# Runs of keys copied by GpSimd for two pairs of an attention + FFN kernel, with a replanned order

## The chip, the cores and the metric

The kernel runs on 1 core of one Trainium2 chip. The metric is the device time of one execution in microseconds (us): the time of the whole program on that core, as the median of several executions. The profiled execution also has a span, from its first to its last instruction; the time of the execution is a little longer than its span.

## What is computed

```python
# q, k, v: (4, 8, 768, 64); x: 3072 tokens x 512; w_in: 512 x 2048; w_out: 2048 x 512
k_sum = k.reshape(B, H, nb, 32, D).max(axis=3)      # nb = 24 blocks of 32 keys
v_sum = v.reshape(B, H, nb, 32, D).mean(axis=3)
scores_l = scale * q @ k^T, masked to |i - j| < 16
scores_s = scale * q @ k_sum^T + log(32)
a = softmax(concat([scores_l, scores_s]))
attn = a @ concat([v, v_sum])
x = attn as 3072 tokens x 512
h = x @ w_in
r = maximum(h, 0)
out = (r * r) @ w_out
```

Each query sees a window of near keys and one maximum per block of 32 keys. The attention's output feeds a squared-ReLU FFN. Everything is float32.

## The kernel before

**Tiling.** The 3072 tokens are cut into 48 groups of 64 queries (g = 0 to 47; 12 groups per batch), and from group 8 on two groups form a *pair* that is handled together: pair n holds groups 2n and 2n + 1, so pair 4 (the fifth) is groups 8, 9 and pair 5 (the sixth) is groups 10, 11. Both still belong to the first batch. Eight groups form a unit of 512 tokens; the FFN runs unit by unit (u = 0 to 5) over 16 slices f of the hidden size. Units 0 and 1 use plain products (L1345 for h, L1369 for the output); units 2 and 3 (L1655, then L1987) and 4 and 5 (L1806, then L1987) use products in Strassen's manner, with sums of weights kept in DRAM (`scr_s`, `scr_a`, `scr_i`, `scr_t`). Each FFN matrix is split into a high and a low float32r part, so a slice takes 12 matmuls of 128x512 in either direction.

**Attention.** `first_attention` handles groups 0 to 7 one by one: scores into PSUM, softmax on VectorE (DVE) and ScalarE (ACT), four transposes on TensorE (PE, L1007), then the values product (L1148). The block maxima (`kb[:, :, :24]`) must stand just ahead of a group's near keys, so GpSimd (POOL) moves them along after every group (`move`, L874, the planner's task KC); the next group's scores wait for that. Pairs are scored by `pair_scores` (L866): 8 heads x 2 halves x 2 groups, 32 products. For batches 1 to 3 the keys lie in DRAM as runs of 88 columns (32 near keys, 24 maxima, 32 near keys, and so on; kG), so a product reads 88 columns in one. For batch 0 (pairs 4 and 5) the maxima and the near keys lie apart, and `pair_keys` gives two pieces: 24 columns of maxima and 64 (or 2x32) near ones. In the order printed below a product is one MATMUL; the trace counts two records for each of them.

After its scores a pair's softmax runs on DVE and ACT, a DVE transpose fills `ta`, four DMAs store it (`turn<-ta`, L1116, task TW), two fetch it in another layout (`a<-turn`, L1124, task TR), and `visit` multiplies it with the values `v` (L1148). There are two buffers for `v` and two for `q`: the loads for the next pair can only start when the former pair's product has read them (`v<-vS`, L789, four DMAs per pair; `q<-qW`, L770, two).

**Order.** Nothing is ordered by hand. Every step is a task with an engine, a key, a cost, what it comes after and which buffers it takes; `Plan.order` simulates the five engines and emits the tasks in the order in which it starts them. The keys come from tables of numbers (`V_LEAD`, `Q_LEAD`, `VISIT_AT`, `KEEP_AT` and so on). Each engine then runs its own instructions in that order, so an instruction that waits holds back all that follow on its engine. All large transfers are issued by one queue, SyncE's (SP); in the program each DMA there waits, besides for its buffers, for the landing of the one eight places before it. The planner before models a transfer as size / 350 GB/s + 1.9 us after the one before, with a table of lateness (`FIRST_LATE`, `LATE`, `V_LATE`, `TR_LATE` and others).

**Weights of the products.** The chunks for L1987 (256 KB each, `w<-scr_a` and `w<-scr_s`, L1955, task CL) go through eight buffers, `wc`. These are places in converted weights, and in unit 2 the last slices of w_in pass through the same eight (`w<-scr_i`, L1606). A chunk load waits until the product that used its buffer is done.

The lines of before that the prediction names: L603 (block maxima of batch 0, DVE), L874 (move, POOL), L796 (copies of sums, POOL), L1281 and L1295 (conversion of weights on ACT), L1014 (copy of a transposed group, ACT), L1574 (`scr_t<-ci`, a store that waits for DVE), L1955, L770, L789.

Of the kernel before, what the change touches and what calls it, by code (L numbers as in the profile page):

```python
# [20 lines left out]
P = 128  # L21
# [42 lines left out]
)  # L64
Q_LEAD = (
# [3 lines left out]
)  # L69
K_LEAD = 73.42, -9.39, -21.49  # L70
TURN_LEAD = (
    1.51, 4.56, 10.36, 0.83, 0.32, -8.81, 19.45, 17.4, -0.53, 9.71, 8.55, -3.09, -4.94, -6.08, -5.46, -8.9, 0.58,
    20.88, 25.32, 5.2, 8.61, 23.24, 12.81, 19.17,
)
HOST_LEAD = (
    12.28, 4.72, 24.43, 38.91, 32.55, 26.28, 29.81, 14.47, -2.7, 5.84, 12.88, 18.8, 17.55, 14.9, 24.8, 22.66,
    16.06, 19.05, 26.89, 29.23, 21.55, 15.39, 32.19, 34.21, 42.91, 20.4, 27.32, 21.21, 36.11, 17.94, 3.66, -12.09,
)
CHUNK_LEAD = 21.45, 27.16, 28.13, 33.44
BLOCK_LEAD = 2.026  # L80
T0 = 28.0
SLOW = 6.007
STEP = 5.855
LEAD = 1.289
FIRST_STEP = 4.02, 3.16
BLOCK_STEP = 1.201
PRODUCT_STEP = 1.32, 1.53, 1.23, 1.04
A0 = 8.649
A1 = 1.909
B0 = 12.893  # L90
B1 = 2.229
HALF_AT = 31.92, 32.59
SECOND = 0.868
IN_AT = 182.63, 270.39, 82.72, 80.5, 255.98, 198.36, 397.3, 399.37
EARLY_SUM = 20.914
# [5 lines left out]
FIRST_LAG = 21.218  # L101
ONE_EXP = 1
LAG = 1.549
# [3 lines left out]
FV_LEAD = -0.72  # L107
FV1_LEAD = -8.476
# [3 lines left out]
TR_LATE = 1.732  # L112
V_LATE = 0.738
FIRST_W_LATE = 2.5
SOON_X = 1.804
SOON_W = 0.262
FIRST_S_KEY = -70.0
FIRST_VM = -60.0, 1.5, 2.5
IL_LATE = 2.513
SUMS_AT = 304.121  # L120
# [72 lines left out]
class Plan:  # L193
# [3 lines left out]
    HOP, DMA_LATENCY, DMA_RATE = 0.12, 1.9, 350e3  # L197
    OWN_LATENCY = 2.5
# [9 lines left out]
    def add(self, name, engine, cost, emit, key, after=(), take=(), use=(), size=0, begin=0.0, behind=None, late=0.0):  # L208
        t = Task(name, engine, cost, emit, key, [a for a in after if a is not None], list(take), list(use), size, begin)
        t.behind, t.late = behind, late  # L210
        t.index = len(self.tasks)
        self.tasks.append(t)
        for b in t.take + t.use:
            b.users.append(t)
        return t

    def order(self):
# [13 lines left out]
        events, n, pipe = [], 0, 0.0  # L231
# [19 lines left out]
        while events:  # L251
# [12 lines left out]
            for e, tasks in ready.items():  # L264
# [1942 lines left out]
```

## Time and profile before

| | |
|---|---|
| median of 3 runs | 591.32 us (589.09 to 592.77) |
| profiled execution, its own time | 589.62 us |
| its span | 587.9 us |
| PE busy | 569.5 us (97%) |
| DVE busy | 438.7 us (75%) |
| ACT busy | 361.7 us (62%) |
| POOL busy | 22.7 us (4%) |
| TensorE clock granted, mean | 0.997 of full speed |
| DMA moved | 156.20 MB, mean 266 GB/s |

PE is the engine to read: it is busy nearly all the time, so what shortens the kernel is fewer matmuls or less time in which PE has nothing to do. A busy time of matmuls is modelled at its ends, and they overlap: in a steady stream a 128x512 matmul shows 0.39 us while the next one starts some 0.227 us later (4 in 1.07 us, 12 in 2.72 us). Idle time on PE stands in square brackets in a timeline, with what ended it.

### The profile page before, as it was taken

The numbers are of one execution on the slowest core, as the hardware profiler recorded it, in microseconds if no ns is written. First come the engines' busy times: TensorE is split into PE (matmuls) and PEld (weight loads), VectorE is DVE, ScalarE is ACT, GpSimd is POOL, SyncE is SP. The second block draws the span as 40 slices with busy tenths as digits, with TensorE's granted clock in tenths as the row PEclk, the third lists the DMA queues.
The fourth block names the chain that finished last, engine by engine and source line by source line (L and its number), as shares of the span: only waits on it lengthen the run. The fifth ranks groups of instructions, "written<-read, shape, count | busy, mean of one in ns | idle before, by whom it ended". The sixth has DMA issues, their size and how long they took to land.

```text
span 587.9 us, 12572 instructions
## 1 busy us (share of the span) xinstructions
PE 569.5 (97%) x4614; PEld 463.9 (79%) x4614; DVE 438.7 (75%) x731; ACT 361.7 (62%) x825; POOL 22.7 (4%) x76
## 2 busy tenths in 40 slices
PE   8879999999999999999899999999999999999997
PEld 6677888888888888888677877788888888788885
DVE  5879999787874787776787978899935623897653
ACT  2979896766654546474663657565547856755542
POOL 4700000000000000000000010000000000000000
PEclk9989999999999999999999999999999999999999
DMA  8995888989699558989998998996899865467672
GB/s 306 369 394 168 294 271 283 316 291 302 222 277 384 177 143 258 341 273 330 353 307 259 291 286 267 296 275 209 248 334 374 280 197 159 148 192 234 195 228 98
DMA packets 101517, 156.20 MB, mean 266 GB/s; under 512 B 9888, under 2 KB 61088, under 8 KB 101456
## 3 DMA queue, kind: packets, MB, share of 16 engines
q1 hardware_dynamic: 101200, 155.00, 81.6%
q8 instruction: 37, 0.61, 0.4%
q0 software_dynamic: 256, 0.39, 0.2%
q14 instruction: 24, 0.20, 0.1%
HBM read 110.40 MB, written 44.56 MB: 264 GB/s over the span
## 4 chain that ended last, share of the span: by engine, by line
PE 75%; DMA 16%; SPq 3%; DVE 3%; ACT 2%; issue 1%; DVEq 0%
PE o L1987 17%; PE o L1369 14%; PE h L1345 14%; PE o L1806 12%; PE end L1987 7%; PE h L1655 5%; DMA raw<-wW 3%; PE x L1148 3%; DMA w<-scr_a 3%; PE att L866 2%; DMA ci<-scr_i 2%; DMA v<-vS 2%; DMA qvpa_lent<-vF 2%; DMA scr_i<-w 1%; DMA q<-qW 1%; DMA fv_lent<-vS 1%
## 5 line engine op out<-in xcount | busy, mean ns | idle before, releaser
L1971 ACT CAST gh<-g 128x512 fp32r<-128x512 f32 x112 | 69.5, 623 | 59.7 <-PE o L1987 29.7
L1976 DVE TENSOR_TENSOR gl<-g,gh 128x512 fp32r<-128x512 f32 x112 | 75.7, 687 | 20.0 <-ACT gh L1971 19.9
L1987 PE MATMUL o<-gh,w 128*128 128x512 f32 x320 | 86.6, 392 | 2.5 <-DMA w<-scr_a 2.5
L1345 PE MATMUL h<-xh,w 128*128 128x512 f32 x240 | 74.8, 392 | 0.8 <-DVE w L1298 0.8
L1987 PEld LDWEIGHTS o<-gh,w 128*128 128x128 f32 x320 | 59.4, 188 | 15.7 <-ACT gh L1971 3.3
L1655 PE MATMUL h<-xh,w 128*128 128x512 f32 x224 | 70.0, 394 | 0.4 <-ACT r L1665 0.4
L1369 PE MATMUL o<-w,gh 128*128 128x512 f32 x240 | 61.6, 393 | 0.0
L1345 PEld LDWEIGHTS h<-xh,w 128*128 128x128 f32 x240 | 44.7, 188 | 10.7 <-DVE w L1298 1.2
L1369 PEld LDWEIGHTS o<-w,gh 128*128 128x128 f32 x240 | 44.6, 188 | 9.6
L1067 ACT ACTIVATE p<-p,nm 128x88 f32<-128x88 f32 x120 | 42.9, 359 | 14.1 <-DVE nm L1061 14.1
L1987 PE MATMUL o<-gl,w 128*128 128x512 f32 x160 | 49.3, 389 | 0.0
L1655 PEld LDWEIGHTS h<-xh,w 128*128 128x128 f32 x224 | 41.4, 188 | 9.9 <-ACT r L1665 0.8
L1345 PE MATMUL h<-xl,w 128*128 128x512 f32 x120 | 46.7, 389 | 0.0
L1655 PE MATMUL h<-xl,w 128*128 128x512 f32 x112 | 43.6, 389 | 0.0
L1665 ACT ACTIVATE r<-h 128x512 f32<-128x512 f32 x32 | 19.1, 595 | 36.9 <-PE h L1655 35.3
L1987 PEld LDWEIGHTS o<-gl,w 128*128 128x128 f32 x160 | 30.0, 188 | 6.3
L1806 PE MATMUL o<-w,w 128*128 128x512 f32 x140 | 34.5, 390 | 0.0
L1987 PE MATMUL end<-gh,w 128*128 128x512 f32 x128 | 34.5, 390 | 0.0
L1354 ACT ACTIVATE r<-h 128x512 f32<-128x512 f32 x30 | 17.9, 597 | 26.3 <-PE h L1345 26.2
L1369 PE MATMUL o<-w,gl 128*128 128x512 f32 x120 | 33.6, 389 | 0.0
L1964 DVE TENSOR_TENSOR g<-g 128x512 f32<-128x512 f32 x48 | 32.5, 684 | 0.8
L1806 PEld LDWEIGHTS o<-w,w 128*128 128x128 f32 x140 | 26.2, 188 | 5.9 <-DVE u L1838 0.5
(212 smaller groups left out, 1051.4 us busy)
## 6 DMA issues: line engine op xcount, KB each, us to landing
raw<-wW SPq DMA_DIRECT2D x32, 512.0 KB, 6.9
w<-scr_s SPq DMA_DIRECT2D x64, 256.0 KB, 3.2
w<-scr_a SPq DMA_DIRECT2D x48, 256.0 KB, 3.2
w<-scr_i SPq DMA_DIRECT2D x38, 256.0 KB, 5.0
scr_t<-ci SPq DMA_DIRECT2D x16, 512.0 KB, 5.9
turn<-ta SPq DMA_DIRECT2D x80, 96.0 KB, 3.7
a<-turn SPq DMA_DIRECT2D x40, 192.0 KB, 3.9
w<-scr_t SPq DMA_DIRECT2D x28, 256.0 KB, 5.4
```

The costliest lines, as they stand in the source:

```text
L1067: nc.scalar.activation(x, x, AF.Exp, bias=nm.tile[:, n : n + 1], accum_out=nm.tile[:, H + n : H + n + 1])
L1148: nc.tensor.matmul(x_of(i)[h % 2 * D : (h % 2 + 1) * D, h // 2, :], lhsT=v_bufs[g].tile[:rows, h * D : (h + 1) * D], rhs=av[:rows, 2 * c : ...
L1345: nc.tensor.matmul(cut(h), lhsT=lhs.tile[:, k * P : (k + 1) * P], rhs=rhs[:, k, c0 : c0 + n], start=(i == 0), stop=(i == 3 * KT - 1),)
L1354: t2 = add(f"RL{name}", "ACT", act, lambda: nc.scalar.activation(cut(r), cut(h), AF.Relu), due + 3, [t1], take=[r], use=[h])
L1369: nc.tensor.matmul(o_of(o, t), lhsT=terms[i][0].tile[:, (t - t0) * P : (t - t0 + 1) * P], rhs=terms[i][1].tile, start=(first and i == 0), ...
L1655: nc.tensor.matmul(h.tile, lhsT=lhs.tile[:, k * P : (k + 1) * P], rhs=rhs[:, k, c0 : c0 + TU], start=(i == 0), stop=(i == 3 * KT - 1),)
L1665: t2 = add(f"RL{name}", "ACT", 0.56, lambda: nc.scalar.activation(r.tile, h.tile, AF.Relu), due + 3, [t1], take=[r], use=[h])
L1806: nc.tensor.matmul(o.tile[:, bank], lhsT=chunk.tile[:, w * HALF + d * P : w * HALF + (d + 1) * P], rhs=xs[y][d], start=starts and i == 0, ...
L1964: lambda x=x, ins=ins, op=op: nc.vector.tensor_tensor(out=x.tile, in0=ins[0].tile, in1=ins[1].tile, op=op),
L1971: f"GH{s}_{n}", "ACT", 0.54, lambda x=x, gh=gh: nc.scalar.copy(out=gh.tile, in_=x.tile), due - 4, ready,
L1976: lambda x=x, gh=gh, gl=gl: nc.vector.tensor_tensor(out=gl.tile, in0=x.tile, in1=gh.tile.bitcast(F32), op=ALU.subtract),
L1987: nc.tensor.matmul(o[d].tile if isinstance(o, tuple) else o.tile[:, d], lhsT=chunk.tile[:, w * HALF + d * P : w * HALF + (d + 1) * P], rhs ...
```

## The change

Three things are changed.

1. **Runs of keys.** For pairs 4 and 5, `first_run` lets GpSimd copy near keys and maxima into runs of 88 columns, as the other batches have them: four copies per pair (task KR). Those of pair 4 go to free columns behind the keys, once the four maxima (L603) are there; those of pair 5 go over the front of the keys, once groups 0 to 3 are scored and moved. `pair_keys` then gives one piece for each product.
2. **The planner.** It no longer models a transfer by one rate and a table of lateness. A DMA takes 0.44 us to issue, at most eight are open at a time, each costs by its count of packets and their size over 16 engines, with 1.2 us before and 1.0 us behind. The `late` numbers go, `dmas=(count, KB)` comes.
3. **The order.** All tables of numbers are new, so every engine's order is new.

```diff
-    HOP, DMA_LATENCY, DMA_RATE = 0.12, 1.9, 350e3
-    OWN_LATENCY = 2.5
+    HOP, HOP_PE = 0.13, 0.22
+    ENGINES, QUEUED, DMA_ISSUE = 16, 8, 0.44
+    PACKET, PER_KB = 0.006, 0.044
+    BEFORE, BEHIND = 1.2, 1.0
+    OWN_LATENCY = 4.5
...
+                if e == "SP" and len(landed) >= self.QUEUED and landed[-self.QUEUED] > now + 1e-9:
+                    free[e] = landed[-self.QUEUED]
...
-                elif t.size:
-                    pipe = max(pipe, end) + t.size / self.DMA_RATE
-                    end = pipe + self.DMA_LATENCY + t.late
+                if e == "SP":
+                    end, (count, kb) = now, t.dmas
+                    work = t.size / 1024 / kb * (self.PACKET + self.PER_KB * kb) / self.ENGINES / count
+                    for _ in range(count):
+                        if len(landed) >= self.QUEUED:
+                            end = max(end, landed[-self.QUEUED])
+                        end += self.DMA_ISSUE
+                        pipe = max(pipe, end + self.BEFORE) + work
+                        landed.append(pipe + self.BEHIND)
...
+    def first_run(pair, free):
+        lo = keys[:, NPAIR * (NB + S) + SQ :][:, : NPAIR * FIRST_RUN].rearrange("p (n k) -> p n k", n=NPAIR)
+        x = first_runs[pair] = lo if free else kb[:, :, NB : NB + FIRST_RUN]
+        k0 = NB + 2 * TQ * pair - WINDOW
...
+        def copy():
+            nc.gpsimd.tensor_copy(out=x[:, :, :SQ], in_=near[:, :, k0 : k0 + SQ])
+            nc.gpsimd.tensor_copy(
+                out=view(x, [[RUN, 2], [1, 2 * SQ]], SQ + NB), in_=view(near, [[2 * SQ, 2], [1, 2 * SQ]], k0 + SQ)
+            )
+            for i in range(2):
+                nc.gpsimd.tensor_copy(out=x[:, :, i * RUN + SQ : i * RUN + SQ + NB], in_=kb[:, :, :NB])
...
     def pair_keys(g, p, half, rows):
 
         b, w = divmod(g, NW)
-        if b:
-            at = w * RUN + half * SQ
-            return [((0, [[1, COLS]]), kg[rows, p, at : at + COLS])]
-        k0 = NB + TQ * w - WINDOW + half * SQ
-        near = keys[rows, p * (NB + S) + k0 : p * (NB + S) + k0 + HALF_W]
-        sums = kb[rows, p, :NB]
-        if half:
-            return [((0, [[1, NB]]), sums), ((NB, [[1, HALF_W]]), near)]
-        return [((SQ, [[1, NB]]), sums), ((0, [[SQ + NB, 2], [1, SQ]]), near.rearrange("p (i k) -> p i k", i=2))]
+        x, at = (kg, w * RUN) if b else (first_runs[g // 2], g % 2 * RUN)
+        return x[rows, p, at + half * SQ : at + half * SQ + COLS]
...
+    def key_runs():
+        for i, pair in enumerate(range(UG // 2, NW // 2)):
+            after = [t_S[3][0], t_KC[3]] if i else []
+            t_KR[pair] = [add(f"KR{pair}", "POOL", 1.25, first_run(pair, not i), RUNS_AT[i], [*t_K[0], t_ends, *after], begin=RUNS_AT[i])]
...
-IN_AT = 182.63, 270.39, 82.72, 80.5, 255.98, 198.36, 397.3, 399.37
+IN_AT = 230.45, 178.82, 256.9, 245.39, 276.31, 334, 389.48, 426.44
```

**What moves: PE at the end of the first eight groups.** `att` is the values product of a group, `t_` a group's transposes, `o_67<-kb,q` the scores of pair 4, `h_0a` the first half-width matmuls of the FFN. Before, with the scores' last two rows at the top:

```order
L866 MATMUL o_67<-kb,q_375 32x24
L866 MATMUL o_67<-kb,q_375 32x64
L1148 MATMUL att<-qvpa_lent 64x64 x8
L1007 MATMUL t_648<-first,qvpa_lent 128x128 x4
L1007 MATMUL t_659<-first,qvpa_lent 128x128 x4
L1148 MATMUL att<-qvpa_lent 64x64 x16
L1345 MATMUL h_0a<-xh,w_0_677 128x256 x2
```

and now:

```order
L1040 MATMUL t_558<-first,qvpa_lent 128x128 x4
L892 MATMUL o_67<-kb,q_383 32x88 x16
L892 MATMUL o_67<-kb,q_386 32x88 x16
L1181 MATMUL att<-qvpa_lent 64x64 x8
L1040 MATMUL t_619<-first,qvpa_lent 128x128 x4
L1378 MATMUL h_0a<-xh,w_0_538 128x256 x2
...
L1040 MATMUL t_656<-first,qvpa_lent 128x128 x4
L1181 MATMUL att<-qvpa_lent 64x64 x16
L1378 MATMUL h_1a<-xh,w_1_662 128x256 x2
```

The scores of a pair are 32 products instead of 64, and the twelve matmuls of `h_0a` stand ahead of the last group's transposes and values product instead of behind them.

**What moves: POOL at the start.** `kb<-kb 128x4x24` at L874 (now L900) are the moves of the maxima, the first of them after group 0's scores. Before:

```order
L586 MEMSET a_80 32x2x256 x2
L932 MEMSET qvpa_lent 128x4x10 x4
L1037 MEMSET p_79 128x8x8
L932 MEMSET qvpa_lent 128x4x10 x4
L874 COPY kb<-kb 128x4x24 x3
```

and now:

```order
L596 MEMSET a_80 32x2x256 x2
L965 MEMSET qvpa_lent 128x4x10 x3
L1070 MEMSET p_79 128x8x8
L965 MEMSET qvpa_lent 128x4x10
L866 COPY kb<-kb 128x4x32
L867 COPY kb<-kb 128x4x2x64
L871 COPY kb<-kb 128x4x24 x2
L900 COPY kb<-kb 128x4x24
```

The four copies of pair 4's run stand ahead of the first move; those of pair 5 stand at the end of POOL's work for the first groups.

**What moves: SP around the first chunks of products.** `kb<-kG` are the keys of the last batch (four DMAs of 544 KB), `w<-scr_i` the last slices of w_in, `w<-scr_a` the chunks. Before:

```order
L789 DMA v_78<-vS 64x512
L599 DMA kb<-kG 128x1088 x4
L1955 DMA w_952<-scr_a_106 128x512
L1955 DMA w_952<-scr_a_107 128x512
L1116 DMA turn_90<-ta_3439 32x3x256 x4
L1508 DMA scr_i_118<-w_908 128x1024
L1955 DMA w_956<-scr_a_108 128x512
L1955 DMA w_956<-scr_a_109 128x512
L1574 DMA scr_t_134<-ci_0_3248 256x2x256
L1574 DMA scr_t_134<-ci_1_3361 256x2x256
L1955 DMA w_1068<-scr_a_110 128x512
```

and now:

```order
L609 DMA kb<-kG 128x1088 x4
L1157 DMA a_80<-turn_87 96x2x256 x2
L799 DMA v_77<-vS 32x512
L799 DMA v_77<-vS 64x512
L1639 DMA w_910<-scr_i_126 128x512
...
L1607 DMA scr_t_132<-ci_1_3241 256x2x256
L1639 DMA w_840<-scr_i_129 128x512 x2
L1149 DMA turn_90<-ta_3369 32x3x256 x4
L1989 DMA w_910<-scr_a_106 128x512
L1989 DMA w_910<-scr_a_107 128x512
```

The keys of the last batch no longer stand directly ahead of the first chunk; between them are now nine other rows, seven loads of w_in's halves among them. They may be loaded once the scores of the pair before are done; between those and the first scores that read them stood 78 wide matmuls on PE, and now stand 84.

## Rows read from the trace of the kernel before

**Rows 1.** Busy time by stretch: us, busy us (instructions) of each engine, PEclk, DMA share, GB/s.
```profile
0.00:36.87 36.87, 29.42 (x486) 22.61 (x486) 25.07 (x61) 21.23 (x80) 17.61 (x66) 0.98 0.96 347
260.00:404.50 144.50, 138.65 (x1320) 111.40 (x1318) 119.22 (x199) 84.80 (x198) 3.09 (x6) 1.00 0.93 290
404.50:588.00 183.50, 179.06 (x792) 147.22 (x788) 114.49 (x177) 105.28 (x176) 0.00 (x0) 1.00 0.70 221
```

**Rows 2.** Waits of PE between 260 and 404 us: total us, times, longest.
```profile
PE o L1987 <- DMA w<-scr_a: 2.5, 2, 1.6
PE att L866 <- DMA q<-qW: 1.1, 1, 1.1
PE x L1148 <- DMA v<-vS: 1.0, 2, 0.6
PE x L1148 <- DMA w<-scr_i: 0.8, 1, 0.8
```

**Rows 3.** Timeline of PE: start, duration, line, operation [idle before, releaser].
```profile
63.95 1.67 PE L866 MATMUL att<-kb,q 64*32 64x24 f32 x128
104.78 0.96 PE L866 MATMUL att<-kb,q 64*32 64x88 f32 x64
```

**Rows 4.** Timeline of PE, end of the first eight groups.
```profile
35.59 1.35 PE L1148 MATMUL att<-qvpa_lent 118*64 118x64 f32 x22 [1.64 <-issue]
36.87 0.80 PE L1345 MATMUL h_0a<-xh,w 128*128 128x256 f32 x2
```

**Rows 5.** Busy time by stretch (as Rows 1) while ACT works on groups 1 to 7.
```profile
15.60:33.60 18.00, 14.89 (x352) 11.74 (x354) 14.57 (x40) 16.35 (x67) 10.29 (x24) 1.00 1.02 370
```

**Rows 6.** Timeline of ACT near the end of the first groups.
```profile
30.23 0.72 ACT L1281 ACTIVATE t<-raw 128x512 f32<-128x512 f32 x1
32.54 1.09 ACT L1014 COPY qvpa_lent<-t 128x512 f32<-128x512 f32 x2
33.52 0.62 ACT L1295 CAST w<-t 128x512 fp32r<-128x512 f32 x1
```

**Rows 7.** Timelines of DVE and POOL in the first 25 us.
```profile
9.65 0.94 DVE L603 TENSOR_REDUCE kb<-kb 128x24 f32<-128x768 f32 x1
11.15 0.27 POOL L874 COPY kb<-kb 128x96 f32<-128x96 f32 x1 [3.53 <-PE o L832]
17.89 1.72 POOL L796 COPY qvpa_lent<-fv_lent 24x512 f32<-24x512 f32 x3
23.72 0.64 DVE L996 TENSOR_TENSOR qvpa_lent<-qvpa_lent,nm 128x472 f32<-128x472 f32 x1
23.77 0.72 POOL L874 COPY kb<-kb 128x96 f32<-128x96 f32 x1 [0.64 <-PE o L832]
```

**Rows 8.** Timeline of PE: the scores of group 1.
```profile
11.98 0.63 PE L832 MATMUL o<-kb,qvpa_lent 64*64 64x118 f32 x16
```

**Rows 9.** Timeline of PE at a wait for queries and one for values.
```profile
312.03 1.02 PE L866 MATMUL att<-kb,q 64*32 64x88 f32 x64 [1.13 <-DMA q<-qW]
374.81 1.39 PE L1148 MATMUL x<-a,v 128*64 128x64 f32 x32 [0.62 <-DMA v<-vS]
```

**Rows 10.** Timeline of SP's issues at the same places (duration: of the issues).
```profile
286.57 1.36 SPq L1574 DMA_DIRECT2D scr_t<-ci  x2
288.02 4.80 SPq L1955 DMA_DIRECT2D w<-scr_a  x5
305.49 1.44 SPq L770 DMA_DIRECT2D q<-qW  x2
```

**Rows 11.** Issue to landing of q (250 to 345 us, 14 DMAs) and v (300 to 345, 9).
```profile
DMA to landing us min/median/max: 3.3/4.3/6.4
...
DMA to landing us min/median/max: 4.7/5.3/6.7
```

**Rows 12.** Timeline of PE: the last two visits of before, 24 wide matmuls apart.
```profile
396.75 1.15 PE L1148 MATMUL x<-a,v 128*64 128x64 f32 x32
403.50 1.15 PE L1148 MATMUL x<-a,v 128*64 128x64 f32 x32
```

More of the change, by code (lines that the diff above doesn't have):

```diff
@@ L100 @@
 )
-FIRST_LAG = 21.218
+FIRST_LAG = -16.679
 ONE_EXP = 1
-LAG = 1.549
+LAG = 2.227
 PLAIN = 2
@@ L206, in __init__, with add @@
         self.tasks = []
-    def add(self, name, engine, cost, emit, key, after=(), take=(), use=(), size=0, begin=0.0, behind=None, late=0.0):
+    def add(self, name, engine, cost, emit, key, after=(), take=(), use=(), size=0, begin=0.0, behind=None, dmas=(1, 2)):
         t = Task(name, engine, cost, emit, key, [a for a in after if a is not None], list(take), list(use), size, begin)
-        t.behind, t.late = behind, late
+        t.behind, t.dmas = behind, dmas
         t.index = len(self.tasks)
@@ L878, in keys_of @@
         b, w = divmod(g, NW)
-        return [t_QL[g]] + ([t_KC[g - 1]] if 0 < g < UG else [t_K[b][p] for p in pairs])
+        return [t_QL[g]] + ([t_KC[g - 1]] if 0 < g < UG else t_KR[g // 2] if not b and g >= UG else [t_K[b][p] for p in pairs])
     def first_attention(g):
@@ L915, in first_pair @@
         t_s = add(
-            f"S{both[1]}", "PE", 1.1, lambda: pair_scores(both), wanted(both[0]) - 15,
-            keys_of(both[0], range(NPAIR)) + [t_QL[both[1]], t_ends], take=s_bufs[g], use=[q_bufs[g] for g in both],
+            f"S{both[1]}", "PE", 0.75, lambda: pair_scores(both), wanted(both[0]) - 15,
+            keys_of(both[0], range(NPAIR)) + [t_QL[both[1]]], take=s_bufs[g], use=[q_bufs[g] for g in both],
         )
@@ L1126, in pair_softmax @@
         t_w = add(
-            f"TW{g}", "SP", 1.75, store, due - 8.5, [t_t], take=[d], use=[ta], size=6 * P * DM
+            f"TW{g}", "SP", 1.75, store, due - 8.5, [t_t], take=[d], use=[ta], size=6 * P * DM, dmas=(4, 1),
         )
@@ L1131, in pair_softmax @@
             t_z.append(add(f"AZ{g}", "POOL", 1.1, lambda: clear_a(a.tile), fetch_at - 8, take=[a], begin=fetch_at - 20))
-        t_a = add(f"TR{g}", "SP", 0.8, fetch, fetch_at, [t_w, t_clear, *t_z], take=[a] * (not t_z), use=[d] + [a] * len(t_z), size=6 * P * DM, behind=last_of("turn", None), late=TR_LATE if both[0] >= NW * 2 else 0.0)
+        t_a = add(f"TR{g}", "SP", 0.8, fetch, fetch_at, [t_w, t_clear, *t_z], take=[a] * (not t_z), use=[d] + [a] * len(t_z), size=6 * P * DM, behind=last_of("turn", None), dmas=(2, 1))
         last_of("turn", t_a)
@@ L1215, in visit @@
         t_v = add(
-            f"V{both[-1]}", "PE", 0.54 * n + 0.11 * (n == 1) + (0.36 if then and then[0] >= NW else 0.49) * len(then) + 0.4 * bool(block_sums), products, due, deps,
+            f"V{both[-1]}", "PE", 0.54 * n + 0.11 * (n == 1) + 0.36 * len(then) + 0.4 * bool(block_sums), products, due, deps,
             take=take, use=use,
@@ L1536, in combine_in @@
             if kept:
-                t = add(f"IL{p}_{k}", "SP", 0.45, load, due - 8 + 0.1 * k, [t_WI[f]], take=[x], size=8 * P * DM, begin=due - 14, behind=behind, late=IL_LATE)
+                t = add(f"IL{p}_{k}", "SP", 0.45, load, due - 8 + 0.1 * k, [t_WI[f]], take=[x], size=8 * P * DM, begin=due - 14, behind=behind, dmas=(1, 4))
                 t_claim.append(t)
@@ L1580, in combine_in @@
             t4 = add(f"IW{p}_{k}", "DVE", 0.6, low, due + 3 + 0.1 * k, [t3], use=[pair[k]])
-            ts.append(add(f"IS{p}_{k}", "SP", 0.45, store, due + 4 + 0.1 * k, [t4], use=[pair[k]], size=8 * P * DM))
+            ts.append(add(f"IS{p}_{k}", "SP", 0.45, store, due + 4 + 0.1 * k, [t4], use=[pair[k]], size=8 * P * DM, dmas=(1, 1)))
         t_IN[p] = ts
```

131 lines of the change are left out of this document (69 added, 62 removed), and 12 rows, old and new, of tables (Q_LEAD, V_LEAD).

## Prediction

> **What bounds the kernel now.** I read the busy time by stretch first. PE is the engine that decides, but not in the same way everywhere [rows 1]. In the first 36.87 us it handles 486 small matmuls and follows ACT and DVE. From there on the wide matmuls run one behind another, and in the last stretch, from 404.50 us on, all 786 of them stand in one block: 786 x 0.227 = 178 us of the 179.06 that PE is busy. Nothing the new order does there can gain anything. Between 260 and 404.5 us the picture is another: PE loses 5.85 us (144.50 less 138.65) while the DMA engines are 93% busy. Who was late says the list of PE's waits for that stretch [rows 2]: chunks of weights 2.5 us, queries 1.1, values 1.0, and a further 0.8 at a values product that hangs on the same queue of loads. Every one ends on a DMA. What can be gained is therefore in three places: the first 37 us, these waits, and the matmuls that are saved.
>
> Both programs have the same 2,136 wide and 48 half-width matmuls by their orders, so only what lies between those counts.
>
> **The change, term by term.** The sum is made against the profiled execution's own 589.62 us (span 587.9); the three runs have their median 1.70 us higher, so a gain is counted from the low end of them.
>
> *Scores of pair 5.* 64 products become 32, with twice the columns or more. The trace has both forms: pair 5 takes 1.67 us now, a pair of a later batch 0.96 [rows 3]. 24 and 64 columns cost as much for each product as 88. The block stands alone between wide matmuls, so the difference is on the path: **-0.7**. Pair 4's scores lie in the first stretch and are in its term.
>
> *GpSimd's copies.* Pair 4's copies wait for the fourth maximum, which DVE ends at 9.65 + 0.94 = 10.6 us [rows 7]; in the new DVE order it stands one place earlier, ahead of a 0.40 us subtraction, so about 10.3. Their prices: 96 columns 0.27 us, 512 columns 1.72 / 3 = 0.57 [rows 7]; four copies of 128, 512, 96 and 96 columns come to 0.3 + 0.57 + 2 x 0.27 = 1.4 us, until 11.7. Behind them stands the first move, which ran at 11.15 [rows 7]: it comes 0.55 us late and ends at about 12.0. Who waits for it is group 1's scores, and these started at 11.98 because other products (sums of values) stand ahead of them on PE in both orders [rows 8]. So the copies cost **0.0**, covered by those products; without that cover 0.55. Pair 5's copies stand behind all moves, some 30 us ahead of their use, and cost nothing.
>
> *The end of the first groups.* Before, the last values product has a hole of 1.64 us in its middle for which the trace names no releaser, and the wide stream starts at 36.87 [rows 4]. Now the twelve half-width matmuls of `h_0a`, 1.4 us, run ahead of the last transposes, in time that PE spent waiting. In return ACT must convert that slice's weights earlier: one rebias (0.72) and two casts (0.62 each) move ahead of the last group's copy, 1.96 us, and that copy ended at 32.54 + 1.09 = 33.6 [rows 6]. ACT was busy for 16.35 of the 18 us before [rows 5], so 1.65 us of the work may fall into its idle time: the copy ends between 33.9 and 35.6. I take 34.5. The values product follows in 1.15 us, so PE enters the stream at 35.8 with 1.4 us of it done: 36.87 - 35.8 + 1.4 = 2.5 us, less 0.3 for one more change between small and wide matmuls and 0.2 for my rounding: **-2.0**. Best, with all idle time filled, -3.0; worst, with none filled and the 1.64 us hole again, +0.7.
>
> *Chunks.* The 2.5 us come from SP, not from bandwidth alone. The first chunk was issued right behind 2.2 MB of keys; a later one was issued at 288.02, behind two `scr_t` stores at 286.57 that wait for DVE [rows 10]. Now the keys stand far ahead, and the buffer of the first chunk is free 3 x 12 wide matmuls and a pair (8.2 + 2.2 us) before its use; before, it was 8.2. The worst landing of a q load there was 6.4 [rows 11]. I take **-2.2** of the 2.5, with 0 and 2.5 as bounds.
>
> *Queries.* The loads that made PE wait 1.13 us at 312.03 [rows 9] were issued at 305.49 [rows 10], some 2.7 us after their buffer was free, behind a store and two chunks. PE has the same 30 wide matmuls between the two pairs now, but SP has only `turn` and `scr_t` stores ahead, which may wait too. **-0.7** of 1.1 (bounds 0 and 1.1).
>
> *Values in the middle.* The four loads of one visit were split around weights and fetches; now they stand together. **-1.0** of the 1.2 us that remain of the 1.0 and 0.8 without the wait at 374.81 [rows 2, 9] (bounds 0 and 1.2).
>
> *New narrow gaps.* The new order sets some visits closer. The last two are 18 wide matmuls apart (4.1 us) and were 24, which took 403.50 - 396.75 = 6.75 us without a wait [rows 12]; two others are 24 apart where 30 brought the wait of 0.62 us at 374.81 [rows 9]; queries get 24 wide matmuls at two places that had 36. A visit's loads take four issues, about 2.2 us, and then 4.7 to 6.7 [rows 11]; from the release in the visit to the next one there are 4.9 us at the tightest place. With landings near the lower bound, as late as this stage is: 0.7 + 0.5 + 0.5 = **+1.7**. Bounds 0 and +7.5 (the second rival).
>
> The planner's rule itself costs no time on the chip.
>
> Sum: 589.62 - 0.7 - 2.0 - 2.2 - 0.7 - 1.0 + 1.7 = **584.7 us**, 1.1% under the median.
>
> [...]
>
> **The rivals.**
>
> *Waits come back in other places (slower than before).* One mechanism: in the busy stage loads land at the slow end. The point is a landing above 4.8 us for queries: 24 wide matmuls and the change are 5.7 us, two issues take 0.9. At 6.4 us (and 5.8 for values) the places cost 0.6 + 2.0 + 1.8 + 3.1 = 7.5 instead of 1.7, and the chunks lose their 2.2 again: 584.7 + 5.8 + 2.2 = 592.7. For it: 93% busy DMA engines [rows 1] and those very landings [rows 11]. Against it: the last gap of 24 went without a wait [rows 12].
>
> *The waits only move.* The planner's new prices do not fit the chip better, and as much is lost in the middle as before; the saved scores and the start remain: 589.62 - 0.7 - 2.0 = 586.9. For it: SP issues in order, and the stores ahead of the loads still wait for DVE.
>
> *All waits go.* Landings near the lower bounds of [rows 11] and the start at its best: -1.7 for the gaps, -0.9 for the remains of three terms, -1.0 for the start: 581.1.
>
> *GpSimd and DVE hold each other up.* A move took 0.72 us instead of 0.27 where it met a DVE multiplication of two SBUF tiles that took 0.64 [rows 7]. If each of the four copies meets one, they take 4 x 0.45 = 1.8 us more, the first move ends at 13.8 and not at 12.0, and the scores and all behind them start that much later: 584.7 + 1.8 = 586.5. Against it: up to 11.7 us DVE does reductions and subtractions that read PSUM. [...]
>
> **How the numbers follow.** Chances: forecast 0.45 (its own range 581.5 to 587.5), slower rival 0.18, all waits go 0.17, waits only move 0.14, the port 0.06. Under 578 I see 0.07, above 592 about 0.12, so the range is 578 to 592. What differs by less than 1% a measurement of this kernel hardly tells from no change. Faster by over 1% is below 585.4: two thirds of the forecast's chance, all of the third rival and some of the rest, 0.53. Slower by over 1% is above 597.2: only the slow mechanism with more places than I counted, 0.07. The rest, 0.40, is the same.
>
> **What would show it.** In the changed kernel's trace pair 5's scores take about 0.96 us and 64 records. The first move on POOL ends by 12.0 us and group 1's scores start at 12.0. The wide stream without a break starts near 35.8 us and not after 37.5. In PE's waits `w<-scr_a` falls under 0.5 us and `q<-qW` under 0.5; the waits for `v<-vS` stand in the last visits and are about 1.5 us. The last block of wide matmuls takes 178 to 179 us as before, so its start tells the whole gain: about 400 instead of 404.6. The prediction is wrong if new waits on DMA in the middle add up to more than 4 us, if ACT ends the last group's copy after 36 us, or if the hole in the first groups turns out to come with every execution.

## The result and the profile after

The changed kernel took 582.93 us in the median of 4 runs (581.41 to 583.19), the kernel before 592.05 of 4 (589.09 to 593.68): a ratio of 0.985, interval 0.980 to 0.989. Forecast were 584.7 us, range 578.0 to 592.0. Two later groups of runs of the same two kernels gave 0.987 (0.982 to 0.993) and 0.986 (0.982 to 0.990). The profiled execution is one of 582.88 us with a span of 581.1; against 587.9 that is 6.8 us less. The medians lie 9.1 us apart; the profiled execution of before was one of the shorter ones (589.62).

Busy time by stretch of the changed kernel, columns as in [rows 1]:

```profile
0.00:35.02 35.02, 28.82 (x434) 22.00 (x434) 26.15 (x64) 21.99 (x82) 20.23 (x74) 1.00 0.96 348
260.00:399.40 139.40, 136.88 (x1229) 110.47 (x1227) 113.47 (x189) 81.59 (x189) 3.07 (x6) 1.00 0.92 288
399.40:581.00 181.60, 176.61 (x779) 144.90 (x774) 112.58 (x175) 103.73 (x174) 0.00 (x0) 1.00 0.73 220
```

The wide stream goes through without small matmuls from 35.02 us on, where it started at 36.87 [rows 1], and twelve of its matmuls are done by then. In the middle stretch PE lost 5.85 us and now loses 139.40 - 136.88 = 2.52. PE's four largest waits from 60 to 399.4 us (total us, times, longest), which answer to [rows 2]:

```profile
PE att L892 <- DMA q<-qW: 0.9, 1, 0.9
PE o L2021 <- DMA w<-scr_a: 0.9, 1, 0.9
PE h L1688 <- ACT r L1698: 0.7, 1, 0.7
PE h L1688 <- ACT fv L759: 0.4, 1, 0.4
```

The timeline of PE at the marks by which the stages are told apart below (answers to [rows 3, 4, 12]):

```profile
34.41 0.69 PE L1181 MATMUL att<-qvpa_lent 118*64 118x64 f32 x16 [0.25 <-ACT qvpa_lent L1047]
35.02 0.51 PE L1378 MATMUL h_1a<-xh,w 128*128 128x256 f32 x2
...
60.23 0.96 PE L892 MATMUL att<-kb,q 64*32 64x88 f32 x64
...
398.37 1.15 PE L1181 MATMUL x<-a,v 128*64 128x64 f32 x32
399.45 1.19 PE L2021 MATMUL o<-gh,w 128*128 128x512 f32 x4
```

Pair 5's scores are 64 records of 0.96 us in all; they were 128 of 1.67. To compare programs with different orders I cut each trace at two equal counts of wide matmuls: the end of the 132nd (the start of the small products behind it, 63.95 before, 60.23 now), and the point with 786 left (404.58 before; now 399.45 less 12 x 0.227 = 396.73, as the last visit has 774 behind it in the new order and 12 are counted over). The stages by this cut, us, for all traces taken (one trace for each row; the programs below before_again are explained with their experiments):

| kernel (span) | to the 132nd | middle | rest | stop of PE without a releaser |
|---|---|---|---|---|
| before (587.9) | 63.95 | 340.63 | 183.33 | 1.64 at 33.95 |
| before_again (593.0) | 62.98 | 346.67 | 183.35 | 1.37 at 33.89 |
| chunks_first (588.5) | 63.45 | 341.81 | 183.27 | 1.37 at 33.76 |
| keys_only (586.9) | 61.33 | 342.27 | 183.30 | none |
| order_only (585.4) | 62.99 | 337.86 | 184.52 | 1.93 at 34.21 |
| fewer_warm (583.2) | 62.48 | 336.71 | 184.03 | 0.53 at 35.93 |
| split_runs (584.4) | 62.58 | 337.03 | 184.77 | 1.66 at 34.07 |
| pair5_old (586.4) | 60.44 | 342.64 | 183.31 | 1.86 at 64.32 |
| h0a_late (582.7) | 60.93 | 337.25 | 184.54 | none |
| after (581.1) | 60.23 | 336.50 | 184.36 | none |
| after_again (583.5) | 61.28 | 338.31 | 183.87 | 0.29 at 30.68 |
| after_third (585.0) | 60.95 | 338.88 | 185.12 | none |
| queries_early (582.3) | 60.35 | 337.90 | 184.09 | none |
| fixed (580.4) | 60.56 | 336.37 | 183.48 | none |

So of the 6.8 us between the two profiled executions 3.7 came before the 132nd wide matmul and 4.1 in the middle, and 1.0 was given back at the end.

What makes the middle long or short can be read from the same traces. Take from it PE's waits (idle times of over 0.1 us) and half of the time at a granted clock of 0.50 (an estimate of what that clock costs: in before three half-width matmuls took 0.64 us from 38.11 us on, at 0.50, and 0.36 from 41.19 us on, at 1.00), and 332.8 to 334.9 us are left in all fourteen. Waits and clock together come to 5.8, 12.6 and 7.7 us in three traces of the old order (before, before_again, keys_only), to 3.0 in order_only and to 3.1, 5.3 and 6.0 in the three of the changed kernel. So the middle's gain is in PE's waits and in what the clock costs behind some of them, and it differs by microseconds from one execution to the next.

### The profile page after: what moved, and what is told of

It is laid out like the page before. It is cut to its first block, busy times and chain, and to the rows that moved or that the text cites. A ratio compares the mean times of both kernels' runs of the same rounds, so it can differ in the third digit from the quotient of the medians.

```text
span 581.1 us, 12287 instructions
## 1 busy us (share of the span) xinstructions
PE 566.4 (97%) x4486; PEld 459.8 (79%) x4486; DVE 438.0 (75%) x731; ACT 359.3 (62%) x825; POOL 25.3 (4%) x84
## 4 chain that ended last, share of the span: by engine, by line
PE 78%; DMA 16%; DVE 4%; SPq 1%; issue 1%; ACT 0%; DVEq 0%
PE o L2021 17%; PE o L1402 15%; PE h L1378 14%; PE o L1840 13%; PE end L2021 8%; PE h L1688 5%; PE x L1181 3%; DMA raw<-wW 3%; PE att L892 2%; DMA w<-scr_i 2%; DMA kb<-kG 2%; DMA ci<-scr_i 1%; DMA fv<-vT 1%; DMA fv_lent<-vS 1%; DMA qvpa_lent<-vF 1%; DMA w<-scr_a 1%
## 5 line engine op out<-in xcount | busy, mean ns | idle before, releaser
L1402 PE MATMUL o<-w,gh 128*128 128x512 f32 x240 | 61.7, 393 | 0.0
L1402 PEld LDWEIGHTS o<-w,gh 128*128 128x128 f32 x240 | 44.5, 188 | 9.5
L1840 PE MATMUL o<-w,w 128*128 128x512 f32 x140 | 34.6, 390 | 0.0
L2021 PE MATMUL end<-gh,w 128*128 128x512 f32 x128 | 34.5, 390 | 0.0
L1402 PE MATMUL o<-w,gl 128*128 128x512 f32 x120 | 33.5, 389 | 0.0
```

Of the source, the lines that this page charges most:

```text
L1402: nc.tensor.matmul(o_of(o, t), lhsT=terms[i][0].tile[:, (t - t0) * P : (t - t0 + 1) * P], rhs=terms[i][1].tile, start=(first and i == 0), ...
L1840: nc.tensor.matmul(o.tile[:, bank], lhsT=chunk.tile[:, w * HALF + d * P : w * HALF + (d + 1) * P], rhs=xs[y][d], start=starts and i == 0, ...
L2021: nc.tensor.matmul(o[d].tile if isinstance(o, tuple) else o.tile[:, d], lhsT=chunk.tile[:, w * HALF + d * P : w * HALF + (d + 1) * P], rhs ...
```

## The experiments

The theory at the start was that of the prediction: the order gains, by filling time in the first groups and by loads that come earlier, and the copies save 0.7 us and pair 4's part. Its rivals were that a stop of the first trace was an accident, and that waits only move.

**before_again and after_again: a second trace of each.** No edit.

> The kernel before, unchanged, for a second trace. Theory A, the stops come from the order: the last values product of the first groups has its hole of 1 to 2 us again, the wide stream starts at 36.5 to 37.2 us and its first 2 us run at a granted clock of 0.50, there is a wait of about 0.9 us on DVE near 50 us, and the two waits for chunks of weights between 280 and 296 us come to 2 to 3 us. Theory B, the hole is an accident of one execution: the stream starts near 35.2 us at full clock, and the span is about 585 us.

> The changed kernel, unchanged, for a second trace. Theory A, the gain belongs to the order: stream from 35.0 us (within 0.3), no half clock, waits of TensorE on DMA between 260 and 399 us of 1.0 to 3.0 us, a wait of 0.8 us on DVE at about 429 us, ratio 0.982 to 0.988. Theory B, the first trace was a lucky one: waits on DMA of over 4 us in that stretch and a ratio above 0.990.

Measured: before_again 590.39 us, ratio to the other runs of before 0.998 (0.996 to 1.001); after_again 583.47 us, 0.987 (0.982 to 0.993). The stop came again, at the same place of the program; timeline of PE of before_again:

```profile
33.36 0.53 PE L1148 MATMUL att<-qvpa_lent 118*64 118x64 f32 x10 [0.42 <-DVE xl L1235]
35.26 0.86 PE L1148 MATMUL att<-qvpa_lent 118*64 118x64 f32 x22 [1.37 <-issue]
36.05 0.50 PE L1345 MATMUL h_0a<-xh,w 128*128 128x256 f32 x2
```

The stop comes with the program; the low clock behind it doesn't come every time: at 37 to 40 us the granted clock was 0.64 in the first trace of before and 1.00 in the second (and 0.61 from 36 to 40 us in chunks_first below, which has the order of before in this stage). The middle is no constant either: 340.63 and 346.67 us in the two traces of before, with other waits and, in the second, with the granted clock at 0.50 from 289.5 to 292.9 us and at 0.54 from 357.5 to 361 us. PE's five largest waits between 260 and 410 us in before_again:

```profile
PE h L1655 <- ACT r L1665: 2.5, 2, 1.4
PE o L1987 <- DMA w<-scr_a: 1.8, 1, 1.8
PE x L1148 <- DMA w<-scr_i: 1.7, 1, 1.7
PE x L1148 <- DMA a<-turn: 1.3, 2, 0.8
PE x L1148 <- DMA v<-vS: 0.7, 1, 0.7
```

The queries, 1.1 us in [rows 2], are not among them. What I took for the price of an order was one draw of it.

**keys_only and order_only: the two halves of the change, one at a time.** keys_only is before with the copies put in by hand, everything else in the old order. order_only has the new order, with nothing copied:

```diff
-t_KR[pair] = [add(f"KR{pair}", "POOL", 1.25, first_run(pair, not i), RUNS_AT[i], ...)]
+t_KR[pair] = [add(f"KR{pair}", "POOL", 1.25, lambda: None, RUNS_AT[i], ...)]
```

and `pair_keys` and the products of before.

> The order of before, with the copies added (pair 4's ahead of the first move, pair 5's behind the last) and the two pairs scored in 32 products of 88 columns each. By the forecast pair 5 saves 0.7 us on the path, pair 4 saves 0.9 us of TensorE's time in a stretch that follows ScalarE, of which 0 to 0.9 reaches the end: 0.7 to 1.6 us, ratio 0.997 to 0.999. By the rival in which GpSimd and VectorE hold each other up, the first move ends at 13.8 us, group 1's scores start 1.8 us later, and the time is 1.1 us above before.

> The order of the changed kernel, but without the copies: pairs 4 and 5 are scored from the keys as they lie, in 64 and 128 products as before. If the gain is the order's: the changed kernel's time and 0.7 to 1.6 us, ratio to before 0.984 to 0.990. If the copies carried more than their 0.7 us, above 0.992.

Measured: keys_only 589.50 us, ratio 0.9965 (0.993 to 0.9995); order_only 586.91 us, 0.993 (0.991 to 0.995), beside 591.68 of before and 583.47 of the changed kernel on the same chip. By the medians the copies are worth 2.2 us in the old order and 3.4 in the new, where 0.7 to 1.6 was expected. Each alone is loose (the interval of keys_only is 0.3 to 3.9 us). The table says where: keys_only has no stop and is at its 132nd wide matmul at 61.33 us, order_only has one of 1.93 us and is there at 62.99, no earlier than before_again. PE of keys_only, then the scores of pair 4 in before (with the copies they take 0.96 us):

```profile
30.37 0.69 PE L1165 MATMUL att<-qvpa_lent 118*64 118x64 f32 x16 [1.41 <-ACT xh L1249]
...
33.35 1.15 PE L1165 MATMUL att<-qvpa_lent 118*64 118x64 f32 x32 [0.42 <-DVE xl L1252]
```
```profile
28.35 1.84 PE L866 MATMUL o<-kb,q 64*32 64x24 f32 x128
```

The product behind pair 4's scores starts at 30.37 us, where it was 30.44 in before: PE waits for ACT instead, so the shorter scores alone gain nothing here. What is gained in this stage is the stop, which stood inside the last values product and is gone from it.

But order_only stops at another place of the program than before, between two transposes:

```profile
33.83 0.38 PE L1048 MATMUL t<-first,qvpa_lent 128*128 128x128 f32 x2
36.14 0.38 PE L1048 MATMUL t<-first,qvpa_lent 128*128 128x128 f32 x2 [1.93 <-issue]
```

What the two places have in common is a count. Busy time from the start into the stop, before and order_only (PE's busy time with its matmuls in brackets stands first after the length):

```profile
0.00:34.50 34.50, 28.14 (x464) 21.45 (x465) 23.94 (x60) 21.02 (x80) 17.61 (x66) 1.00 0.96 343
```
```profile
0.00:35.00 35.00, 28.82 (x464) 22.27 (x465) 25.19 (x62) 21.11 (x80) 17.44 (x66) 1.00 0.96 353
```

464 matmuls in both. A new theory: PE had used up the instructions it had. The trace of before has 37 transfers of instructions of 16 KB each (0.61 MB in all) on DMA queue 8, and the DMA engines are 96% busy up to the stop.

**fewer_warm and split_runs: is it the count?** fewer_warm is order_only with a shorter warm-up:

```diff
-nc.tensor.matmul(x.tile, lhsT=ident(), rhs=ident(), start=True, stop=True)
+if i < 8:
+    nc.tensor.matmul(x.tile, lhsT=ident(), rhs=ident(), start=True, stop=True)
```

split_runs is the changed kernel with pair 4's products cut in two:

```diff
+for c0, c1 in ((0, COLS // 2), (COLS // 2, COLS)) if g // 2 == UG // 2 else ((0, COLS),):
+    nc.tensor.matmul(to[:, c0:c1], lhsT=..., rhs=x[:, c0:c1], start=True, stop=True)
```

> The kernel of order_only (new order, no copies) with 12 of the 28 warm-up matmuls left out at the start (their products are used by nobody). If TensorE ran out of instructions, which come in blocks of 16 KB, the hole stays at the same count: after 464 matmuls, which is now 12 products later in the program, inside the values products behind the last transposes, and it ends 1.3 to 1.5 us after a 16 KB transfer of instructions. If it were a wait for data, it stays at the same place of the program: inside the last transposes, after 452 matmuls.

> The changed kernel in which each of pair 4's products of 88 columns is made as two of 44: the copies and the layout of the keys stay, the number of TensorE's instructions is again that of order_only up to that place. If the number of instructions makes the hole: TensorE stops without a releaser after 464 matmuls, for 1 to 2 us, until 1.3 to 1.5 us after a 16 KB transfer of instructions, and the time is 1.5 to 3.5 us above the changed kernel. If the layout of the keys (how they are read) made the difference: no such hole, and the time is 0 to 0.9 us above the changed kernel.

Measured: fewer_warm 584.93 us in one run; split_runs 586.45 us, 0.991 (0.988 to 0.994). PE of fewer_warm, its count up to there, then PE of split_runs and its count:

```profile
34.81 0.60 PE L1049 MATMUL t<-first,qvpa_lent 128*128 128x128 f32 x4
35.38 0.56 PE L1190 MATMUL att<-qvpa_lent 118*64 118x64 f32 x10
36.46 0.91 PE L1190 MATMUL att<-qvpa_lent 118*64 118x64 f32 x22 [0.53 <-issue]
```
```profile
0.00:36.40 36.40, 29.03 (x464) 21.47 (x464) 25.72 (x62) 21.74 (x82) 17.45 (x66) 0.95 0.98 358
```
```profile
29.63 1.59 PE L894 MATMUL o<-kb,q 64*32 64x44 f32 x128 [0.60 <-ACT qvpa_lent L1012]
...
33.69 0.38 PE L1042 MATMUL t<-first,qvpa_lent 128*128 128x128 f32 x2
35.73 0.38 PE L1042 MATMUL t<-first,qvpa_lent 128*128 128x128 f32 x2 [1.66 <-issue]
```
```profile
0.00:35.00 35.00, 28.76 (x464) 22.32 (x465) 25.53 (x62) 21.10 (x80) 20.23 (x74) 1.00 0.97 357
```

With twelve warm-up matmuls fewer the stop stands twelve products later in the program, and again after 464. It is shorter, 0.53 us, as PE came there later. And with the copies in place but twice the products it is back, at 464, and the time is 3.4 us above the 583.09 us of the changed kernel's 14 runs (on other chips). It is not the layout of the keys that counts but how many instructions PE goes through. The DMA records show the rest. Queues of split_runs between 33.3 and 34.6 us:

```profile
q1 hardware_dynamic: 201, 0.48, 96.0%
q8 instruction: 1, 0.02, 5.2%
```

One packet of instructions among 201 of data. The end of the last such packet ahead of each stop, and the time at which PE goes on:

| trace | matmuls done | 16 KB landed | PE goes on | later by |
|---|---|---|---|---|
| before | 464 | 34.23 | 35.59 | 1.36 |
| before_again | 464 | 33.81 | 35.26 | 1.45 |
| chunks_first | 464 | 33.75 | 35.13 | 1.38 |
| order_only | 464 | 34.77 | 36.14 | 1.37 |
| fewer_warm | 464 | 35.00 | 36.46 | 1.46 |
| split_runs | 464 | 34.44 | 35.73 | 1.29 |
| after_again | 338 | 29.65 | 30.97 | 1.32 |
| pair5_old | 718 | 64.71 | 66.18 | 1.47 |

In the changed kernel the packet landed at 34.83 us and PE had its 465th matmul at 40.30: 64 small matmuls fewer lie ahead, and wide ones come in their place, which take 0.12 (half-width) or 0.227 us each where one of pair 4's 128 records took 1.84 / 128 = 0.014. It is a race: in all fourteen traces this packet landed 3.8 to 5.5 us after PE's 339th matmul, 126 ahead of the 465th, and PE passed those 126 in 5.2 us in before, up to its stop, and in 10.5 in the changed kernel. What starts a packet, and why it takes so long, the runs don't show.

**pair5_old: which pair?** Pair 5 alone is scored from the keys as they lie.

```diff
-x, at = (kg, w * RUN) if b else (first_runs[g // 2], g % 2 * RUN)
+if b or g // 2 == UG // 2:
+    (as in the changed kernel)
+(as before)
```

> The changed kernel in which pair 4 keeps its runs of 88 columns and pair 5 is scored from the keys as they lie, in 128 matmul records. If the hole of 1.4 to 1.9 us after the 464th matmul comes from pair 4's burst of small matmuls: no hole of over 0.6 us without a releaser before 37 us, pair 5's scores take 1.67 us, the time is 0.7 us above the changed kernel (ratio to before 0.984 to 0.990). If the hole hangs on the total number of instructions or on pair 5: a hole of 1 to 2 us, and 2.5 to 3.5 us above.

Measured: 585.45 us, 0.989 (0.984 to 0.994), 132nd wide matmul at 60.44 us: in its trace pair 4's copies alone take the first stop away. But in the profiled execution pair 5's 128 records led into a stop of their own, behind four wide matmuls:

```profile
60.44 1.67 PE L900 MATMUL att<-kb,q 64*32 64x24 f32 x128
62.04 1.15 PE L1190 MATMUL x<-a,v 128*64 128x64 f32 x32
63.12 1.20 PE L1411 MATMUL o<-w,gh 128*128 128x512 f32 x4
66.18 1.20 PE L1411 MATMUL o<-w,gh 128*128 128x512 f32 x4 [1.86 <-issue]
```
```profile
67.00:69.00 2.00, 2.00 (x7) 1.56 (x6) 2.00 (x3) 0.00 (x0) 0.00 (x0) 0.58 0.99 392
```

After it the clock is 0.58 for 2 us. That execution is the 588.13 us one of six between 584.30 and 590.34; how often this stop comes is open. The two traces of before, with the same 128 records at that place, don't have it.

**h0a_late: did `h_0a` fill idle time?** One task is emitted behind another (`FI0_0a` behind `V7`).

> The changed kernel with one move: the twelve half-width matmuls of h_0a stand behind the last values product of the first groups, as in the order of before. By the forecast they filled time in which TensorE waited: the 132nd wide matmul comes 1.1 to 1.5 us later than in the changed kernel (60.2 and 61.3 us in two traces), the whole time is 1 to 1.5 us longer. By the rival they only pushed the last transposes back, and the place costs 0 to 0.4 us.

Measured: 584.14 us, 0.987 (0.983 to 0.992), and the 132nd wide matmul at 60.93, inside the 60.23 to 61.28 of the three traces of the changed kernel. These differ by what came before, so the start of pair 4's scores is the better mark. From there to the 132nd it takes 31.30 us in h0a_late and 30.80 to 30.82 in after, after_third, queries_early, fixed and pair5_old (31.30 also in after_again, which has a stop of 0.29 us in between): the place is worth 0.5 us. The last transposes of h0a_late, then of the changed kernel, PE:

```profile
32.85 0.63 PE L1040 MATMUL t<-first,qvpa_lent 128*128 128x128 f32 x4 [1.06 <-ACT qvpa_lent L1047]
```
```profile
32.84 0.60 PE L1040 MATMUL t<-first,qvpa_lent 128*128 128x128 f32 x4
```

So `h_0a` did fill time in which PE otherwise waits for ACT, 1.06 us of it, and PE came to its first matmul of L1402 at 38.50 us instead of 39.65. But of the 1.1 to 1.5 us forecast only 0.5 is left at the 132nd. Neither side of the expectation is quite met, and the times of the whole kernel don't resolve half a microsecond.

**chunks_first: are the chunks late by SyncE's order?** In the order of before, `KL3_0` to `KL3_3` (keys) are moved ahead of `QL36`, and `IS4_0`, `IS4_1` (the scr_t stores) behind `CL0_7`.

> The kernel before with two moves on SyncE's queue: the four loads of batch 3's keys stand right behind the scores that free their tile (ahead of two queries, three loads of values and a fetch), and the two scr_t stores that stood between the chunks stand behind the eighth chunk. By the forecast (SyncE's order makes the chunks late) the waits for chunks of 2.5 and 1.8 us in the two traces of before fall to 0 to 0.8 us and the time by 1.5 to 2 us, ratio 0.996 to 0.998. By the rival (the DMA engines are full whatever the order) they stay at 1.8 us or more.

Measured: 593.23 us, 1.002 (0.999 to 1.006). No wait on w<-scr_a is left among PE's waits. At the first chunk PE waits 0.64 us, for ACT, where it waited 1.59 for the chunk, so there the order did make it late (which of the two moves did it is not shown). At the second PE now stands for another reason, so this trace says nothing of it. DVE has something behind the stores: a subtraction into their buffer, and behind that `gl`, for which PE waits. DVE, then PE:

```profile
294.93 0.69 DVE L1532 TENSOR_TENSOR ci<-w 128x512 f32<-128x512 f32 x1 [6.49 <-DMA scr_t<-ci]
...
296.47 0.68 DVE L1976 TENSOR_TENSOR gl<-g,gh 128x512 fp32r<-128x512 f32 x1
```
```profile
292.42 1.07 PE L1987 MATMUL o<-gh,w 128*128 128x512 f32 x4
297.21 0.73 PE L1987 MATMUL o<-gl,w 128*128 128x512 f32 x2 [3.72 <-DMA v<-vS]
```

3.7 us lost for at most 2.5 gained (the releaser that the profile infers for PE is not the true one here: `gl` was written from 296.47 to 297.15). In time no gain is seen.

**after_third, queries_early and fixed: is there more to have?** queries_early moves two loads of queries (`QL42`, `QL43`) ahead of loads of weights (`HL3_8_0`) on SyncE's queue. fixed also moves a load of queries (`QL39`) behind the eighth chunk (`CL0_7`), an exponential of ACT (`E43`) behind `VS3`, and a subtraction of DVE (`IR6_0`) behind `C00_1_1`.

> The changed kernel, unchanged, beside the two that follow on the same chip: 582 to 584 us. No hole without a releaser of over 0.6 us before 37 us; the wait for queries near 315 us between 0.5 and 2.3 us; the waits for chunks at most 1.1 us.

> The changed kernel with one move on SyncE's queue: the two loads of queries for which TensorE waits near 315 us stand ahead of two loads of the w1 ring and a load of values' sums, so that they are issued as soon as their buffers are free (0.9 us earlier in the trace). If the order of the loads makes them late: the wait of 0.9 to 2.3 us falls to 0 to 0.6, the time by 0.7 to 1.5 us. If the full DMA engines do: they land later than 5 us after the issue and 0.7 us or more stays.

> The changed kernel with the move of queries_early and three more: one load of queries behind the eighth chunk of weights, an exponential of ScalarE behind the copy of the values' sums for which TensorE waits near 331 us, and a subtraction of VectorE that waits for a load near 429 us behind the addition for which TensorE waits. Each takes away a wait that most traces of the new order show (0 to 1.1, 0.9 to 2.3, 0.4 to 1.0, 0.2 to 1.1 us): 1.5 to 3 us faster than the changed kernel, 579.5 to 582 us. If the waits only move, within 0.7 us of it.

Measured on one chip: after_third 584.31 us (0.986), queries_early 584.16 (0.987), fixed 584.45 (0.986; interval 0.982 to 0.989). No difference between the three is seen. The queries are in time now: their loads land 2.5 to 3.3 us after issue, and were 5.4 to 5.6. What stood ahead of them, a load of values, lands later, and DVE waits for it with `xl` behind. DVE and then PE of queries_early:

```profile
318.43 0.95 DVE L747 TENSOR_REDUCE fv<-fv 128x24 f32<-128x768 f32 x1 [0.74 <-DMA fv<-vT]
...
319.90 0.68 DVE L1268 TENSOR_TENSOR xl<-x,xh 128x512 fp32r<-128x512 f32 x1
```
```profile
320.63 0.73 PE L1688 MATMUL h<-xh,w 128*128 128x512 f32 x2 [0.88 <-DVE xl L1268]
```

In fixed the waits for chunks, for `fv` and at 429 us are gone from the trace (waits of 1.4 us for `xl` are left), its span of 580.4 is the shortest, and its median is still that of the changed kernel. Whether single waits of 0.5 to 1 us are worth anything here can't be told from six runs each that spread over 3 to 7 us.

## Why the prediction came out as it did

The time, 582.93, lies 1.8 us under the 584.7 and inside the range and the forecast's own range. The way there was in part another one, and by one sign that the prediction named for itself it was wrong: the stop in the first groups came in every traced execution with the order and the products of before (before, before_again, chunks_first).

*Scores of pair 5, -0.7.* Right: 1.67 to 0.96 us. (A product with 88 columns isn't as cheap as an old one, as I read: 0.96 / 32 = 0.030 against 1.67 / 64 = 0.026 us. The difference of the blocks stands.) What I left out is what 64 matmuls fewer mean for the supply of instructions.

*GpSimd's copies, 0.0.* Right, and better than said. Timeline of POOL and, last, of PE:

```profile
8.84 0.29 POOL L866 COPY kb<-kb 128x128 f32<-128x128 f32 x1 [1.48 <-DMA kb<-kT]
9.07 0.61 POOL L867 COPY kb<-kb 128x512 f32<-128x512 f32 x1
9.93 0.48 POOL L871 COPY kb<-kb 128x96 f32<-128x96 f32 x2 [0.24 <-DVE kb L613]
10.41 0.27 POOL L900 COPY kb<-kb 128x96 f32<-128x96 f32 x1
```
```profile
11.70 0.64 PE L842 MATMUL o<-kb,qvpa_lent 64*64 64x118 f32 x16
```

Their prices come to 1.38 us (1.4 forecast), but I let all four wait for the fourth maximum. The two large ones read the loaded keys alone and ran before it, so the first move ends at 10.68 and not at 12.0. The rival in which GpSimd and DVE hold each other up ("the port" in the list of chances) has no place here: none of the four was drawn out. Of pair 5's copies the first was, 0.75 us instead of 0.29 at 24.88 us, where nothing waits for it.

*The end of the first groups, -2.0 (bounds -3.0 to +0.7).* The size is near, the step behind it failed. To the 132nd wide matmul the stage is 3.72 us shorter between the two first traces, and 1.7 to 3.7 over two traces of before and three of the changed kernel. ACT's copy ended at 34.4 (34.5 forecast), but `h_0a` in PE's waiting time, which was to bring nearly all of it, is worth 0.5 us (h0a_late). The 0.3 us for one more change between small and wide matmuls was an estimate that no run shows as such; [rows 12] leave 6.75 - 1.15 - 24 x 0.227 = 0.15 us for the two at a visit. I read the 1.64 us of [rows 4] as a thing that might or might not recur, and gave it no term. It was the term: a stop for instructions, which pair 4's 64 extra matmuls bring about (order_only, split_runs) and the copies remove (keys_only). By keys_only the copies shorten this stage by 1.7 to 2.6 us. Part of the rest in the first trace of before is the low clock behind the stop (0.50 from 36.87 to 39.0 us), which its second trace didn't show; a further 0.78 is a wait for converted weights at 51.7 us (0.75 in before_again), which isn't among the waits of the new order and which I had not put into the sum.

*Chunks, -2.2.* Too large: 2.5, 1.8 and 0.8 us of waits in three traces of the old order (before, before_again, keys_only), 0.9, 0.4 and 1.0 in three of the changed kernel, so about 0.9. That SP's order makes the first chunk late is shown (chunks_first); for the second it stays argued.

*Queries, -0.7.* The wait of [rows 9], with 30 wide matmuls between two pairs, is gone from the changed kernel's traces. But it isn't among the listed waits of before_again and keys_only either, so there was less to gain than one trace said.

*Values, -1.0.* Too small. The products of values waited 1.8, 3.7 and 2.7 us for their loads in the old order (before, before_again, keys_only), and 0, 0 and 0.5 in the changed kernel.

*New narrow gaps, +1.7.* The one for queries cost more than its part: at one of the two places with 24 wide matmuls instead of 36, near 316 us, PE waited 0.9, 2.2 and 2.1 us, and behind the two long waits the granted clock fell (0.53 and 0.54 from 318.2 to 321.8 us, 1.00 in the first trace). At the tightest gap of values, 18 wide matmuls, the loads landed after 2.2 to 3.2 us in the first trace, not 4.7: from 393 to 397 us the DMA engines were 78% busy, and 93% from 300 to 345 us in before, where [rows 11] are taken. In after_third the 0.5 us of the values are at this place. The rival in which all waits go took the whole 1.7 away; [rows 11], with 3.3 and 4.7 us at the least, did not show that, and this wait for queries stayed.

*Not in the sum.* "Every one ends on a DMA" is not so: [rows 2] lack a fifth wait, of 0.4 us for ACT's `r` at L1655. The line of before, from 260 to 404 us:

```profile
PE h L1655 <- ACT r L1665: 0.4, 1, 0.4
```

In before_again and keys_only the waits for `r` come to 2.5 and 3.3 us, in the changed kernel to 0.7, at 255 us, in each of its traces. This gain of the new order had no term. And in the last stage, which I said the new order could not touch, it lost 1.0: DVE stood at a subtraction that waits for a load, with the addition behind it for which PE waits. DVE and PE of the changed kernel:

```profile
429.18 0.69 DVE L1565 TENSOR_TENSOR ci<-ci 128x512 f32<-128x512 f32 x1 [1.34 <-DMA ci<-scr_i]
429.79 0.68 DVE L1872 TENSOR_TENSOR u<-o,u 128x512 f32<-128x512 f32 x1
```
```profile
430.53 1.65 PE L1840 MATMUL o<-w,host 128*128 128x512 f32 x6 [0.77 <-DVE u L1872]
```

The clock had no term either. Its mean over an execution was 0.995 in 59 runs of before and 0.998 in the 14 of the changed kernel; by an estimate from these, 0.003 x 590 = 1.8 us of the gain at the most.

Put together, from the runs: the copies 2.2 to 3.4 us where 0.7 stood, the new order 4.8 by order_only's median, where the terms of the order came to 4.2. The stop that I didn't count (1.7 us or more in the first stage), the waits for values and for `r`, longer than my one trace of before had them, and the clock erred to one side; `h_0a`, the chunks, the narrow gap of queries and the last stage, each by about a microsecond, erred to the other. That the sum fell so near is in part luck.

## What to carry to other kernels

A stop of TensorE with no releaser, after the same number of matmuls in programs of different order, points to a wait for instructions (here the stop came after 464 in six traces of five programs): look whether a transfer of instructions ended just ahead of its end (here 1.29 to 1.47 us), and try with fewer small matmuls ahead of it, even where they stand beside other work and seem free. A load moved ahead in a queue pays with whatever it passes; follow that to its next reader before pricing the move (in the traces of chunks_first and queries_early new waits of 3.72 and 0.88 us stood there, and the one was no faster than before, the other no faster than the changed kernel). Where a stage waits on busy DMA engines, take the waits from two or three traces: here single ones differed between executions of one program by as much as a term of the forecast (the waits for `r` came to 0.4 and 2.5 us in the two traces of before, and the largest term was 2.2).

## What the runs showed of the hardware

Packets of instructions of 16 KB came by DMA on queue 8, beside the data on queue 1: 37 in the trace of before with its 4614 matmuls, 36 in that of the changed kernel with 4486, so one packet fewer with 128 matmuls and their weight loads fewer. TensorE went on 1.29 to 1.47 us after such a packet's end in all eight stops. The stops stand after 338, 464 and 718 matmuls, 126 and 2 x 127 apart. That these packets hold TensorE's instructions is read from the counts and the times; how many a packet holds, the runs don't show.

The granted clock fell to 0.50 of full speed behind some of PE's stops and not behind others. It fell in before (0.50 from 36.87 to 39.0 us, after 1.64 us), chunks_first (0.61 on average from 36 to 40 us, after 1.37) and pair5_old (0.58 from 67 to 69 us, after 1.86), and behind waits for queries of 2.16 and 2.07 us in after_again and after_third (0.53 and 0.54 from 318.2 to 321.8 us). It stayed at 1.00 in before_again after 1.37 us, order_only after 1.93, split_runs after 1.66, and h0a_late after a wait for queries of 2.28. (Where a stretch is longer than the low clock, the figure is its mean.) So the length of the stop alone doesn't decide it; what does, these runs don't show.
